# The second expert pass of an attention, MLP and expert-mixture kernel in hand-written program order

## The chip, the cores and the metric

The kernel runs on one core of a Trainium2 chip, in one launch. The time is device time in microseconds (us). TensorE (PE) multiplies, VectorE (DVE), ScalarE (ACT) and GpSimd (POOL) do the elementwise work, and SyncE (SP) issues the transfers. Each engine takes the instructions of its own queue in the order in which they stand there, and waits for the results of others by semaphores.

## What is computed

```python
x = attention(q, k, v)                 # 4 x 8 heads, 576 tokens, 64 wide; k and v averaged over 8 rows first
h = x @ w_in;  g = where(h > 0, h, exp(min(h, 0)) - 1);  x = g @ w_out       # 2304 x 512, inner 2048
P = exp(x @ w_gate - max);  8 times: P /= P.sum(1); P /= P.sum(0); P *= N / E
for e in range(8):                     # w1[e] 512 x 1024, w2[e] 1024 x 512
    out += P[:, e:e+1] * (np.maximum(x @ w1[e], 0.0) @ w2[e])
```

The change concerns the loop over the eight experts alone.

## The kernel before

Every float32 product is made of three products on a faster type, fp32r: an operand is cast to a high part ("hi", an ACT cast), the rest is subtracted into a low part ("lo", on POOL or DVE), and hi x hi, hi x lo and lo x hi are added up in PSUM. Each expert's two matrix products are blocked two by two and done by a scheme of seven block products with sums of blocks instead of eight.

**Pass 1** (the experts' first layer) runs over 32 pairs, an expert and a quarter of its hidden rows each, and within a pair over three units of 384 token columns. A unit has seven products of six matmuls (`Unit.product`, L810). The names in the trace: `pa` to `pd` are the PSUM banks of products, `m`, `u`, `r`, `s` the tiles that `Unit.read` makes of them, `w` the weights (`w10_31` is the high, `w11_31` the low half of pair 31's), `xs` the tokens. The results `r` and `s` are written to DRAM (`hid`) by `keep`, seven blocks of a unit. `split_pair(i)` makes a pair's weights: four sums and three subtractions (L781) on POOL, three casts on ACT (L780).

**The second pass** (the experts' second layer) runs over 72 pairs: 8 experts x 3 units x 3 blocks of 128 tokens. A pair has seven products of twelve matmuls 128x256 (`Pair.product`, L987), in the order a, b, then the seventh product of the pair before (c), then a, b, c, d. `prepare` makes a product's operands from the hidden blocks `hl` that come back from DRAM: the cast g (L954), in three of seven products a copy `pg` into PSUM (L957), and the low half g (L960), on POOL for two of the seven and on DVE for the others. It runs four products ahead of TensorE (`AHEAD`). `Pair.read` empties the banks: the copy n (L1014, ACT), the sums v, pc and poc (DVE), and the gated addition into the output tiles `acc` (in expert 0 ACT writes them, L1002; later DVE adds, L1004).

Beside an expert's pairs the next expert's weights are made: `weights_ahead` is a generator, and each call of `advance()`, one for each product of a pair, goes on with it to its next `yield`. `load_w2` fetches four blocks of 512 KB into two tiles `rv`. For each half of the rows there are seven blocks: B11, B22, B21 as they were loaded, and T1 to T4, which are differences of them (`sum_w2`, L906, POOL; three overwrite `rv`, the fourth, T3, has a tile `t3`). Each block is cast (L913, ACT) and its low half subtracted (L915, POOL).

Tiles come from pools: 24 large ones (`slot`: weights, tokens, `hl`, `rv`, `acc`), 13 small ones (`piece`: g, t3, n, v, and in pass 1 m, u, r, s), 8 PSUM banks (`bank`). A tile asked for when all are taken waits for the oldest to be given back. Only the attention's beginning stands in an order written by hand; from there on, in both passes of the experts too, a scheduler sets the order of each engine's queue.

Of the kernel before, what the change touches and what calls it, by code (L numbers as in the profile page):

```python
# [17 lines left out]
def tile_attention_mlp_moe(  # L18
# [31 lines left out]
    nc = tc.nc  # L50
# [30 lines left out]

    cpool = ctx.enter_context(tc.tile_pool(name="cpool", bufs=1))
    spool = ctx.enter_context(tc.tile_pool(name="spool", bufs=24))
    hpool = ctx.enter_context(tc.tile_pool(name="hpool", bufs=13))
    dpool = ctx.enter_context(tc.tile_pool(name="dpool", bufs=1, space=bass.MemoryType.DRAM))
    small = ctx.enter_context(tc.tile_pool(name="small", bufs=3))
    psum = ctx.enter_context(tc.tile_pool(name="psum", bufs=8, space=bass.MemoryType.PSUM))
# [700 lines left out]
    class Unit:  # L788
# [33 lines left out]
        def read(self, m):  # L822
            p = self.bank
            if m == 1:
                self.m1 = self.temp("m1")
                nc.scalar.copy(self.m1, p["a"])  # L826
            elif m == 6:
                self.u2 = self.temp("u2")
                nc.vector.tensor_add(self.u2, p["b"], self.m1)  # L829
            elif m == 2:  # L830
                self.r11 = self.temp("r11")
                nc.scalar.activation(self.r11, p["a"], AF.Relu)
                self.keep(H11, self.r11)
            elif m == 7:
                self.u3 = self.temp("u3")
                nc.vector.tensor_add(self.u3, p["b"], self.m1)
            elif m == 5:
                self.r22 = self.temp("r22")
                nc.vector.tensor_add(self.r22, p["c"], self.u3)  # L839
                nc.scalar.activation(self.r22, self.r22, AF.Relu)  # L840
                self.keep(H22, self.r22)
            elif m == 4:
                self.r12 = self.temp("r12")
                nc.vector.tensor_add(self.r12, p["d"], self.u3)
                nc.scalar.activation(self.r12, self.r12, AF.Relu)
                self.keep(H12, self.r12)
            else:

                c, s2 = p["c"], bank(f"ps_{self.i}_{self.u}")[:, 0:UW]
                s3 = self.temp("s3")  # L850
                nc.vector.tensor_add(c, c, self.u2)
                nc.vector.scalar_tensor_tensor(
                    s3, c, 0.0, self.r11, op0=ALU.max, op1=ALU.subtract
                )
                self.keep(HS3, s3)
                nc.vector.scalar_tensor_tensor(
                    c, c, 0.0, self.r22, op0=ALU.max, op1=ALU.add
                )
                nc.vector.tensor_sub(s2, c, self.r11)
                nc.scalar.copy(self.r22, c)  # L860
                self.keep(HS1, self.r22)
                nc.vector.tensor_sub(self.r12, self.r12, s2)
                self.keep(HS4, self.r12)
                nc.scalar.copy(self.r11, s2)
                self.keep(HS2, self.r11)


    w2s, loaded, prepared, acc = {}, {}, {}, {}
# [4 lines left out]


    B11, T2, B21, T3, T1, T4, B22 = range(7)
    ORDER2 = (1, 6, 2, 7, 5, 4, 3)
    LOADS2 = (range(0, 4), range(4, 7))

# [19 lines left out]
    def sum_w2(e, j, half):  # L898

        a, b = {T3: (T1, B22), T1: (T1, B11), T2: (B22, T1), T4: (B21, T2)}[j]  # L900
        if j == T3:
            out = sums2[e, half] = piece([P, 2, HF], F32, f"t3_{e}_{half}")
        else:
            raw2[e, j] = raw2[e, a]
            out = half_of(raw2[e, j], half)
        nc.gpsimd.tensor_sub(out, half_of(raw2[e, a], half), half_of(raw2[e, b], half))  # L906
# [13 lines left out]
    def weights_ahead(e):  # L920

        load_w2(e)
        for _ in range(8):
            yield
        for half in range(2):
            for j in (B11, B22, T3, B21, T1, T2, T4):
                if j in (T3, T1, T2, T4):
                    sum_w2(e, j, half)
                    yield
                yield from split_w2(e, j, half, nc.gpsimd)  # L930
                yield

    at_chunk2 = [0]

# [253 lines left out]
        while not all(k in made for k in CUTS if k[1] == u):  # L1188
            advance()

    def split_now(j, eng):
        for half in range(2):
            run(split_w2(0, j, half, eng))

    def first_weights(u):

        if u == 0:
            split_now(B11, nc.vector)
            split_now(B22, nc.vector)
            for j in (T3, T1, T2):  # L1200
                for half in range(2):
                    sum_w2(0, j, half)
        elif u == 1:
            del xslots[0]
            load_hidden()
            split_now(T2, nc.gpsimd)
            split_now(B21, nc.vector)
            split_now(T3, nc.gpsimd)
            split_now(T1, nc.gpsimd)
            for half in range(2):  # L1210
                sum_w2(0, T4, half)
        else:
            del xslots[1]
            load_hidden()
            load_hidden()
            split_now(T4, nc.gpsimd)

    def end_pair(p):
        p.product(6)
# [8 lines left out]
    for n, (i, u) in enumerate(order1):  # L1228
        need(u)
        unit = Unit(i, u)  # L1230
        for m in (1, 6, None, 2, 7, 5, 4):
            if m is not None:
                unit.product(m)
                unit.read(m)
            elif last is not None:
                last.product(3)
                last.read(3)
                if last.u == NUNIT - 1:
                    del w1s[last.i]
                if i == len(pairs) - 1:  # L1240
                    first_weights(u)
            advance(2 if len(made) < len(CUTS) else 1)
        last = unit
        if n == 2 * NUNIT - 2:
            need(NUNIT - 1)
            load_pair(2)
            load_pair(3)
        if n >= 2 * NUNIT - 1 and u == NUNIT - 1 and i + 1 < len(pairs):
            split_pair(i + 1)
            if i + 3 < len(pairs):  # L1250
                load_pair(i + 3)
        if (i, u) == (len(pairs) - 2, NUNIT - 1):
            load_w2(0)
    last.product(3)
    last.read(3)
    xslots.clear()
    w1s.clear()


    AHEAD = 4  # L1260
    N2 = len(pairs2)


    order2 = [(n + (j == 6), (0, 1, 3, 4, 5, 6, 2)[j], n, j) for n in range(N2) for j in range(7)]
    order2 = [7 * n + j for _, _, n, j in sorted(order2)]
    coming = iter(order2)
    for _ in range(AHEAD):
        prepare(next(coming))

    def prepare_next():  # L1270
        advance()
        i = next(coming, None)
        if i is not None:
            prepare(i)

    before = None
    for n in range(N2):
        e, u, s = pairs2[n]
        pair = Pair(n)
        for j in (0, 1, None, 2, 3, 4, 5):  # L1280
            if j is not None:
                prepare_next()
                pair.product(j)
                pair.read(j)
            else:
                if before is not None:
                    prepare_next()
                    end_pair(before)
                if e + 1 < E and (u, s) == (0, 0):
                    side.append(weights_ahead(e + 1))  # L1290
        before = pair
    end_pair(before)


# [33 lines left out]
```

## Time and profile before

| | us |
|---|---|
| median of 3 runs | 2031.45 (2029.45 to 2032.22) |
| profiled execution | 2033.06 |
| its span | 2031.30 |
| TensorE busy in it | 1950.4 (96%) |
| VectorE, ScalarE, GpSimd busy | 1360.8, 1101.2, 725.5 |

The second pass takes the span from 1235.8 to the end. The granted clock in the profile is 1 at 2.4 GHz, TensorE's higher level, and is lower where part of a stretch ran at the lower level of 1.2 GHz. A row of the timeline gives in brackets how long the engine had idled before the instruction and which instruction ended the wait; "issue" means that nothing visible did. Instructions follow each other in a pipeline, so a row's own time can reach into the next row's.

### The profile page before, as it was taken

What the parts mean: (1) busy time and instruction counts of PE and PEld (TensorE: products, weight loads), DVE (VectorE), ACT (ScalarE), POOL (GpSimd) and SP (SyncE); (2) the same over time, 40 slices, a digit from 0 to 9 for tenths busy, and PEclk for the clock granted to TensorE, in tenths of its full rate; (3) what the DMA queues carried; (4) which work ended last, traced back from release to release, by engine and by line L of the source; (5) the groups of instructions that cost most, each with busy time, mean ns of one, the idle gap of its engine ahead of it and who ended that gap; (6) DMA issues with size and microseconds to landing.
All of it is one profiled execution on the core that took longest, in us unless ns stands there. A gap on an engine that the chain in (4) does not pass through costs nothing. (4 is left out here: it accounts for less than half of the span.)

```text
span 2031.3 us, 35842 instructions
## 1 busy us (share of the span) xinstructions
PE 1950.4 (96%) x12717; PEld 1851.9 (91%) x12717; DVE 1360.8 (67%) x2586; ACT 1101.2 (54%) x2211; POOL 725.5 (36%) x624
## 2 busy tenths in 40 slices
PE   7799999999999999999999998898999999999999
PEld 4578888888999999999999998898989999999998
DVE  8687878445787666666666665556666666666666
ACT  5665545344444444444444446765666565656654
POOL 6510000020043233233233326645555554546422
PEclk7999999999999999999999999999999999999999
DMA  9221111000256656656656669675767676766691
GB/s 255 72 79 63 63 42 53 1 11 1 99 202 220 212 205 228 211 202 231 213 198 228 220 226 295 171 202 157 212 177 192 182 196 177 204 175 194 195 293 58
DMA packets 440163, 335.84 MB, mean 165 GB/s; under 512 B 25520, under 2 KB 431024, under 8 KB 439984
## 3 DMA queue, kind: packets, MB, share of 16 engines
q1 hardware_dynamic: 439984, 333.56, 53.2%
q8 instruction: 100, 1.64, 0.3%
q14 instruction: 79, 0.65, 0.1%
HBM read 196.62 MB, written 136.84 MB: 164 GB/s over the span
## 5 line engine op out<-in xcount | busy, mean ns | idle before, releaser
L954 ACT CAST g<-hl 128x512 fp32r<-128x512 f32 x504 | 305.2, 620 | 164.0 <-PE pob L987 83.1
L960 POOL TENSOR_TENSOR g<-hl,g 128x512 fp32r<-128x512 f32 x144 | 187.2, 1300 | 335.5 <-ACT g L954 266.0
L987 PE MATMUL pob<-w,g 128*128 128x256 f32 x1728 | 242.0, 291 | 17.1 <-POOL g L960 16.4
L781 POOL TENSOR_TENSOR w<-rw,w 128x512 fp32r<-128x512 f32 (+1 forms) x96 | 140.9, 1499 | 327.2 <-ACT w L780 259.1
L987 PE MATMUL poa<-w,g 128*128 128x256 f32 x1728 | 236.1, 287 | 16.0 <-ACT n L1014 13.5
L987 PEld LDWEIGHTS pob<-w,g 128*128 128x128 f32 x1728 | 227.0, 199 | 18.9 <-POOL g L960 17.9
L987 PE MATMUL poc<-w,g 128*128 128x256 f32 x1728 | 237.1, 287 | 7.1 <-DVE pc L1025 6.8
L987 PEld LDWEIGHTS poa<-w,g 128*128 128x128 f32 x1728 | 221.3, 195 | 18.1 <-ACT n L1014 15.1
L810 PE MATMUL pc<-xs,w 128*128 128x384 f32 x1152 | 231.9, 335 | 2.2 <-DVE r L839 2.2
L810 PE MATMUL pa<-xs,w 128*128 128x384 f32 x1152 | 231.6, 335 | 2.1 <-ACT m L826 2.1
L810 PE MATMUL pb<-xs,w 128*128 128x384 f32 x1152 | 231.2, 334 | 0.3 <-DVE u L829 0.3
L987 PEld LDWEIGHTS poc<-w,g 128*128 128x128 f32 x1728 | 223.0, 196 | 8.7 <-ACT w L913 7.6
L650 PE MATMUL p<-h,w 128*128 128x512 f32 (+1 forms) x960 | 215.9, 372 | 0.4 <-ACT h L638 0.4
L810 PEld LDWEIGHTS pa<-xs,w 128*128 128x128 f32 x1152 | 203.0, 188 | 3.1 <-ACT m L826 3.1
L775 POOL TENSOR_TENSOR rw<-rw 128x256 f32<-128x256 f32 x32 | 23.9, 747 | 507.9 <-DMA rw<-in_moe_w_dram 415.1
L960 DVE TENSOR_TENSOR g<-pg,g 128x512 fp32r<-128x512 f32 x216 | 148.7, 688 | 84.4 <-ACT g L954 39.4
L810 PEld LDWEIGHTS pc<-xs,w 128*128 128x128 f32 x1152 | 201.8, 188 | 3.4 <-DVE r L839 3.4
L810 PEld LDWEIGHTS pb<-xs,w 128*128 128x128 f32 x1152 | 202.2, 188 | 1.4 <-DVE u L829 1.4
L650 PEld LDWEIGHTS p<-h,w 128*128 128x128 f32 x960 | 167.6, 190 | 29.9 <-ACT h L638 0.6
L617 PE MATMUL p<-xh,w 128*128 128x512 f32 x512 | 171.8, 395 | 0.0
L960 DVE TENSOR_TENSOR g<-hl,g 128x512 fp32r<-128x512 f32 x144 | 117.6, 817 | 38.2 <-ACT g L954 15.4
L829 DVE TENSOR_TENSOR u<-pb,m 128x384 f32<-128x384 f32 x96 | 53.4, 557 | 133.1 <-PE pb L810 65.1
(152 smaller groups left out, 3318.4 us busy)
## 6 DMA issues: line engine op xcount, KB each, us to landing
hl<-hid SPq DMA_DIRECT2D x504, 256.0 KB, 5.1
hid<-r SPq DMA_DIRECT2D x576, 192.0 KB, 2.5
hid<-s SPq DMA_DIRECT2D x96, 192.0 KB, 2.1
rw<-in_moe_w_dram SPq DMA_DIRECT2D x128, 128.0 KB, 2.7
rv<-in_moe_w_dram SPq DMA_DIRECT2D x32, 512.0 KB, 6.9
raw<-in_moe_w_in_dram SPq DMA_DIRECT2D x16, 512.0 KB, 4.1
raw<-in_moe_w_out_dram SPq DMA_DIRECT2D x16, 512.0 KB, 11.2
vraw<-in_v_dram SPq DMA_DIRECT2D x16, 288.0 KB
```

Source lines behind the costliest of these rows:

```text
L617: nc.tensor.matmul(ps[:, 0:n], wc[:, 0, a, c * P : (c + 1) * P], b[:, c, :], start=c == 0 and m == 0, stop=c == NC - 1 and m == 2,)
L650: nc.tensor.matmul(ps[j][:, 0 : WIDTH[t]], wc[:, 1, a, j * P : (j + 1) * P], h[b], start=f == 0 and m == 0, stop=f == SIZE[g] - 1 and m == 2,)
L775: g.tensor_sub(raw[:, S3], raw[:, A11], raw[:, A21])
L781: g.tensor_sub(w1s[i][1][:, js], raw[:, rs], f32(w1s[i][0][:, js]))
L810: nc.tensor.matmul(self.bank[b], a[:, c, :], x, start=first and c == 0 and n == 0, stop=c == 1 and n == 2, skip_group_check=not first,)
L829: nc.vector.tensor_add(self.u2, p["b"], self.m1)
L954: nc.scalar.copy(hi, x)
L960: eng.tensor_sub(lo, x, f32(hi))
L987: nc.tensor.matmul(self.bank[b], h[a][:, f, :], w2s[self.e, j][:, l, f, :], start=first and f == 0 and n == 0, stop=f == NPAIR - 1 and n == 2,
```

## The change

Five edits. (1) The second pass stands in a `manual_schedule` block for all five engines: each engine's queue is in the order in which the code issues the instructions. (2) `weights_ahead` has more `yield`s: a sum is followed by two, and a block without a sum has one more at its end, so that 58 steps stand where 44 stood; `load_w2(0)` is called earlier (before `split_pair(31)`). (3) From expert 1 on, T3 goes into the free half of the last output tile (`acc_t3`), not into a piece; the small pool has 14 tiles. (4) The last three results of a unit of pass 1 go to new pieces `s1`, `s4`, `s2` and no longer overwrite r22, r12 and r11. (5) The first expert's weights are a generator stepped once for each step of pass 1's last pair, where they were issued in three lumps, and the operands of the second pass's first four products are prepared ahead of pass 1's last product.

```diff
-    hpool = ctx.enter_context(tc.tile_pool(name="hpool", bufs=13))
+    hpool = ctx.enter_context(tc.tile_pool(name="hpool", bufs=14))
...
                 nc.vector.tensor_sub(s2, c, self.r11)
-                nc.scalar.copy(self.r22, c)
-                self.keep(HS1, self.r22)
-                nc.vector.tensor_sub(self.r12, self.r12, s2)
-                self.keep(HS4, self.r12)
-                nc.scalar.copy(self.r11, s2)
-                self.keep(HS2, self.r11)
+                v = self.temp("s1")
+                nc.scalar.copy(v, c)
+                self.keep(HS1, v)
+                v = self.temp("s4")
+                nc.vector.tensor_sub(v, self.r12, s2)
+                self.keep(HS4, v)
+                v = self.temp("s2")
+                nc.scalar.copy(v, s2)
+                self.keep(HS2, v)
...
         if j == T3:
-            out = sums2[e, half] = piece([P, 2, HF], F32, f"t3_{e}_{half}")
+            if e == 0:
+                out = piece([P, 2, HF], F32, f"t3_{half}")
+            else:
+                out = half_of(spare[0], half)
+            sums2[e, half] = out
...
             for j in (B11, B22, T3, B21, T1, T2, T4):
-                if j in (T3, T1, T2, T4):
+                if j in SUMS:
                     sum_w2(e, j, half)
+                    yield
                     yield
                 yield from split_w2(e, j, half, nc.gpsimd)
                 yield
+                if j not in SUMS:
+                    yield
+
+    spare = []
+
+    def last_acc():
+
+        both = slot([P, SLOT], F32, "acc_t3")
+        half = SLOT // 2
+        acc[NTILE - 1] = both[:, 0:half].rearrange("p (s d) -> p s d", d=DM)
+        spare.append(both[:, half:SLOT].rearrange("p (f d) -> p f d", f=NPAIR))
...
+    def first_weights():
+
+
+        G, V = nc.gpsimd, nc.vector
+        sum_w2(0, T3, 0), split0(B11, None, V)
+        yield
+        sum_w2(0, T3, 1), split0(B11), split0(B22, None, V)
+        yield
+        sum_w2(0, T1, 0), split0(B22)
+        yield
+        sum_w2(0, T1, 1)
+        yield
+        sum_w2(0, T2, 0)
+        yield
+        sum_w2(0, T2, 1)
+        yield
+        yield
+        del xslots[0]
+        load_hidden()
+        split0(T2, None, G), split0(B21, None, V)
+        yield
+        split0(B21), split0(T2, 0)
...
                 if last.u == NUNIT - 1:
                     del w1s[last.i]
-                if i == len(pairs) - 1:
-                    first_weights(u)
+                if (i, u) == (len(pairs) - 2, NUNIT - 1):
+                    load_w2(0)
+                if (i, u) == (len(pairs) - 1, 0):
+                    side.append(first_weights())
...
-        if (i, u) == (len(pairs) - 2, NUNIT - 1):
-            load_w2(0)
-    last.product(3)
-    last.read(3)
...
+    for _ in range(AHEAD):
+        prepare(next(coming))
+
+    last.product(3)
+    last.read(3)
+    xslots.clear()
+    w1s.clear()
+    last_acc()
+
+
+    with tc.manual_schedule(engines={E_.PE, E_.DVE, E_.Activation, E_.Pool, E_.SP}):
+        before = None
+        for n in range(N2):
```

What this does to the queues stands in the order of the two programs. First POOL's queue while the weights of expert 3 are made beside expert 2, in the kernel before: `w2_3_*` are low halves of weights, `rv3_*` sums, `g1_*` low halves of the pairs' operands; a name in brackets is an engine or transfer queue that the instruction waits for.

```order
L960 TENSOR_TENSOR g1_162_16145<-hl23_0_16015,g0_162_16144 128x512 [waits DMAHW5_49,PE_49,Activation_49]
L906 TENSOR_TENSOR t3_3_1_16162<-rv3_0_15513,rv3_6_15516 128x512 [waits DVE_49,PE_49]
L906 TENSOR_TENSOR rv3_0_15513<-rv3_0_15513 128x512 [waits Pool_49]
L906 TENSOR_TENSOR rv3_6_15516<-rv3_6_15516,rv3_0_15513 128x512 [waits Pool_49]
L915 TENSOR_TENSOR w2_3_3_15795<-t3_3_1_16162,w2_3_3_15795 128x512 [waits Activation_49]
L915 TENSOR_TENSOR w2_3_4_15904<-rv3_0_15513,w2_3_4_15904 128x512 [waits Activation_49]
L906 TENSOR_TENSOR rv3_6_15516<-rv3_6_15516 128x512 [waits Pool_49]
L915 TENSOR_TENSOR w2_3_1_15970<-rv3_6_15516,w2_3_1_15970 128x512 [waits Activation_49]
L915 TENSOR_TENSOR w2_3_5_16035<-rv3_6_15516,w2_3_5_16035 128x512 [waits Activation_49]
L960 TENSOR_TENSOR g1_165_16236<-hl23_1_16063,g0_165_16235 128x512 [waits DMAHW0_49,PE_49,Activation_49]
```

The same place of the changed kernel:

```order
L980 TENSOR_TENSOR g1_162_16423<-hl23_0_16294,g0_162_16422 128x512 [waits DMAHW5_49,DVE_49,Activation_49]
L923 TENSOR_TENSOR w2_3_5_16464<-rv3_6_15802,w2_3_5_16464 128x512 [waits DMAHW3_49,DMAHW2_49,Activation_49]
L980 TENSOR_TENSOR g1_165_16513<-hl23_1_16341,g0_165_16512 128x512 [waits DMAHW0_49,DVE_49,Activation_49]
L923 TENSOR_TENSOR w2_3_0_15968<-rv3_0_15799,w2_3_0_15968 128x512
L980 TENSOR_TENSOR g1_169_16573<-hl24_0_16444,g0_169_16572 128x512 [waits DMAHW4_49,DVE_49,Activation_49]
L923 TENSOR_TENSOR w2_3_6_16034<-rv3_6_15802,w2_3_6_16034 128x512
L914 TENSOR_TENSOR acc_t3_13062<-rv3_0_15799,rv3_6_15802 128x512
L980 TENSOR_TENSOR g1_172_16661<-hl24_1_16492,g0_172_16660 128x512 [waits DMAHW7_49,DVE_49,Activation_49]
L923 TENSOR_TENSOR w2_3_3_16137<-acc_t3_13062,w2_3_3_16137 128x512 [waits Activation_49]
L980 TENSOR_TENSOR g1_176_16722<-hl25_0_16595,g0_176_16721 128x512 [waits DMAHW3_49,DVE_49,Activation_49]
L923 TENSOR_TENSOR w2_3_2_16185<-rv3_6_15802,w2_3_2_16185 128x512
L914 TENSOR_TENSOR rv3_0_15799<-rv3_0_15799 128x512
```

Before, eight weight steps stand between g1_162 and g1_165; in the changed kernel no more than two stand between one g1 and the next, and T3's sum (`acc_t3`) waits for nothing.

Then TensorE's queue where pass 1's last pair (31) begins, in the kernel before:

```order
L810 MATMUL pa_31_0_12444<-xs0_0_3974,w10_31_12430 128x384 x2
L810 MATMUL pa_31_0_12444<-xs0_0_3974,w11_31_12431 128x384 [waits Pool_49]
L810 MATMUL pa_31_0_12444<-xs0_0_3974,w10_31_12430 128x384 x2
L810 MATMUL pa_31_0_12444<-xs0_0_3974,w11_31_12431 128x384
L810 MATMUL pb_31_0_12453<-xs0_3_3977,w10_31_12430 128x384 x2
L810 MATMUL pb_31_0_12453<-xs0_3_3977,w11_31_12431 128x384 [waits Pool_49]
L810 MATMUL pb_31_0_12453<-xs0_3_3977,w10_31_12430 128x384 x2
L810 MATMUL pb_31_0_12453<-xs0_3_3977,w11_31_12431 128x384
L810 MATMUL pc_30_2_12404<-xs2_1_4745,w10_30_12190 128x384 [waits DVE_49]
L810 MATMUL pc_30_2_12404<-xs2_2_4746,w10_30_12190 128x384
L810 MATMUL pc_30_2_12404<-xs2_1_4745,w11_30_12191 128x384
L810 MATMUL pc_30_2_12404<-xs2_1_4745,w10_30_12190 128x384
```

The same place of the changed kernel:

```order
L810 MATMUL pa_31_0_12720<-xs0_0_3974,w10_31_12712 128x384 x2
L810 MATMUL pb_31_0_12729<-xs0_3_3977,w10_31_12712 128x384 x2
L810 MATMUL pc_30_2_12686<-xs2_1_4745,w10_30_12457 128x384 [waits DVE_49]
L810 MATMUL pc_30_2_12686<-xs2_2_4746,w10_30_12457 128x384
L810 MATMUL pc_30_2_12686<-xs2_1_4745,w11_30_12458 128x384
L810 MATMUL pc_30_2_12686<-xs2_1_4745,w10_30_12457 128x384
L810 MATMUL pc_30_2_12686<-xs2_2_4746,w10_30_12457 128x384
L810 MATMUL pc_30_2_12686<-xs2_1_4745,w11_30_12458 128x384
L810 MATMUL pa_31_0_12720<-xs0_0_3974,w11_31_12713 128x384 [waits Pool_49]
L810 MATMUL pa_31_0_12720<-xs0_0_3974,w10_31_12712 128x384 x2
L810 MATMUL pa_31_0_12720<-xs0_0_3974,w11_31_12713 128x384
L810 MATMUL pb_31_0_12729<-xs0_3_3977,w11_31_12713 128x384 [waits Pool_49]
```

Before, twelve matmuls of pair 31 stand ahead of pc_30_2, the last product of the pair before. In the changed kernel four stand there, and the others, which need the low half w11_31, stand behind it.

Last ACT's queue ahead of m1_31_2, the copy of the first product of pass 1's last unit, in the kernel before (`w2_0_5` is the cast of T4):

```order
L860 COPY r22_31_0_12523<-pc_31_0_12516 128x384 [waits DMAHW7_49,DVE_49,Activation_49]
L864 COPY r11_31_0_12505<-ps_31_0_12562 128x384 [waits DMAHW1_49,DVE_49]
L840 ACTIVATE r22_31_1_12626<-r22_31_1_12626 128x384 [waits DMAHW4_49,DVE_49]
L845 ACTIVATE r12_31_1_12637<-r12_31_1_12637 128x384 [waits DMAHW5_49,DVE_49]
L826 COPY m1_31_2_12648<-pa_31_2_12641 128x384 [waits PE_49]
L913 CAST w2_0_5_12687<-rv0_6_12441 128x512 [waits Pool_49]
L913 CAST w2_0_5_12687<-rv0_6_12441 128x512
```

The same place of the changed kernel:

```order
L921 CAST w2_0_4_12917<-rv0_0_12663 128x512
L921 CAST w2_0_5_12967<-rv0_6_12666 128x512 [waits PE_49,Pool_49]
L867 COPY s2_31_0_12854<-ps_31_0_12841 128x384 [waits DMAHW2_49,DVE_49]
L832 ACTIVATE r11_31_1_12874<-pa_31_1_12816 128x384 [waits DMAHW5_49,DMAHW7_49,DMAHW3_49,PE_49]
L921 CAST w2_0_5_12967<-rv0_6_12666 128x512 [waits Pool_49]
L826 COPY m1_31_2_12927<-pa_31_2_12920 128x384 [waits DMAHW1_49,PE_49,Activation_49]
L840 ACTIVATE r22_31_1_12899<-r22_31_1_12899 128x384 [waits DMAHW5_49,DVE_49]
```

Before, both casts of T4 stand behind m1_31_2; in the changed kernel both stand ahead of it, each with a wait for POOL.

## Rows read from the trace of the kernel before

**Rows 1.** Page, part 1: busy us, share of the span, instructions of each engine.

```profile
PE 1950.4 (96%) x12717; PEld 1851.9 (91%) x12717; DVE 1360.8 (67%) x2586; ACT 1101.2 (54%) x2211; POOL 725.5 (36%) x624
```

**Rows 2.** Windows by stretch; PE, PEld, DVE, ACT, POOL busy, clock, DMA share, GB/s.

```profile
700.00:1120.00 420.00, 420.00 (x2425) 420.00 (x2424) 271.20 (x520) 199.14 (x404) 140.69 (x137) 1.00 0.61 215
...
1235.80:1250.75 14.95, 11.80 (x72) 11.01 (x73) 7.55 (x15) 9.48 (x20) 3.86 (x3) 0.77 0.96 307
1250.75:1340.57 89.82, 83.55 (x674) 82.40 (x673) 45.08 (x81) 64.77 (x127) 51.28 (x38) 0.98 0.71 199
1340.57:1933.98 593.41, 561.99 (x4538) 558.51 (x4538) 384.80 (x700) 364.47 (x681) 319.44 (x240) 0.97 0.69 189
1933.98:2014.62 80.64, 80.64 (x674) 80.64 (x673) 55.57 (x104) 47.03 (x88) 20.81 (x16) 1.00 0.67 193
```

**Rows 3.** Waits of PE, second pass: us in total, times, longest us.

```profile
PE pob L987 <- POOL g L960: 16.4, 7, 2.9
PE poa L987 <- ACT n L1014: 13.5, 8, 2.3
PE poc L987 <- DVE pc L1025: 6.8, 8, 1.2
```

**Rows 4.** Windows: the 3.4 us behind one wait (columns of the second group).

```profile
1474.90:1478.30 3.40, 3.39 (x17) 3.39 (x18) 2.38 (x5) 1.81 (x4) 3.40 (x3) 0.55 0.48 138
```

**Rows 5.** Timeline of POOL in expert 2: start, us, instruction [idle before it].

```profile
1461.72 1.30 POOL L906 TENSOR_TENSOR t<-rv,rv 128x512 f32<-128x512 f32 x1 [4.15 <-issue]
...
1490.66 1.30 POOL L960 TENSOR_TENSOR g<-hl,g 128x512 fp32r<-128x512 f32 x1 [2.03 <-DVE g L960]
...
1503.05 1.30 POOL L960 TENSOR_TENSOR g<-hl,g 128x512 fp32r<-128x512 f32 x1
```

**Rows 6.** Timeline of ACT and PE, the same stretch, two windows.

```profile
1474.91 2.50 PE L987 MATMUL pob<-w,g 128*128 128x256 f32 x10 [2.58 <-POOL g L960]
...
1500.64 0.62 ACT L913 CAST w<-rv 128x512 fp32r<-128x512 f32 x1 [2.32 <-POOL rv L906]
...
1502.11 1.70 PE L987 MATMUL poa<-w,g 128*128 128x256 f32 x12 [1.73 <-ACT n L1014]
```

**Rows 7.** Groups by line and form, second pass: busy us, mean ns, idle before.

```profile
L960 DVE TENSOR_TENSOR g<-pg,g 128x512 fp32r<-128x512 f32 x216 | 148.7, 688 | 84.4 <-ACT g L954 39.4 <-ACT pg L957 24.9 <-POOL w L915 5.7
...
L960 DVE TENSOR_TENSOR g<-hl,g 128x512 fp32r<-128x512 f32 x144 | 117.6, 817 | 38.2 <-ACT g L954 15.4 <-ACT pg L957 13.9 <-issue 1.6
...
L915 POOL TENSOR_TENSOR w<-rv,w 128x512 fp32r<-128x512 f32 x84 | 115.2, 1386 | 27.1 <-ACT w L913 22.7 <-PE pod L987 2.5 <-issue 1.5
```

**Rows 8.** Waits of ACT in pass 1, of 420 us.

```profile
ACT r L860 <- DMA hid<-r: 19.7, 19, 1.9
```

**Rows 9.** Timeline of POOL, then of PE, end of pass 1.

```profile
1208.85 2.55 POOL L906 TENSOR_TENSOR t<-rv,rv 128x512 f32<-128x512 f32 x2 [13.10 <-ACT r L860]
...
1217.29 1.29 POOL L906 TENSOR_TENSOR rv<-rv,rv 128x512 f32<-128x512 f32 x1 [3.40 <-DVE w L915]
1219.27 1.27 POOL L906 TENSOR_TENSOR rv<-rv,rv 128x512 f32<-128x512 f32 x1 [0.69 <-DVE w L915]
...
1227.67 1.29 POOL L906 TENSOR_TENSOR rv<-rv 128x512 f32<-128x512 f32 x1
...
1212.07 1.20 PE L810 MATMUL pc<-xs,w 128*128 128x384 f32 x6
...
1220.30 1.32 PE L810 MATMUL pc<-xs,w 128*128 128x384 f32 x6 [0.78 <-DVE r L839]
1222.45 1.31 PE L810 MATMUL pa<-xs,w 128*128 128x384 f32 x6 [0.83 <-ACT m L826]
...
1229.84 1.20 PE L810 MATMUL pa<-xs,w 128*128 128x384 f32 x6
```

**Rows 10.** Group of POOL's line L781, wide form.

```profile
L781 POOL TENSOR_TENSOR w<-rw,w 128x768 fp32r<-128x768 f32 x4 | 7.4, 1853 | 41.5 <-ACT w L780 23.6 <-PE pc L810 17.8
```

More of the change, by code (lines that the diff above doesn't have):

```diff
@@ L875, in tile_attention_mlp_moe @@
     B11, T2, B21, T3, T1, T4, B22 = range(7)
+    SUMS = (T1, T2, T3, T4)
     ORDER2 = (1, 6, 2, 7, 5, 4, 3)
@@ L1189, in need, with split0 @@
             advance()
[L1191 to L1216, printed above, removed]
+    splitting = {}
+    def split0(j, half=None, eng=None):
+        for h in range(2) if half is None else (half,):
+            if (j, h) in splitting:
+                run(splitting.pop((j, h)))
+            else:
+                splitting[j, h] = split_w2(0, j, h, eng)
+                next(splitting[j, h])
+    def first_weights():
[18 more added lines that the diff above has]
+        split0(B21), split0(T2, 0)
+        yield
+        split0(T2, 1), split0(T3, None, G)
+        yield
+        sum_w2(0, T4, 0), split0(T3, 0)
+        yield
+        sum_w2(0, T4, 1), split0(T1, None, G)
+        yield
+        split0(T3, 1)
+        yield
+        split0(T1, 0)
+        yield
+        del xslots[1]
+        load_hidden()
+        split0(T1, 1), split0(T4, None, G)
+        load_hidden()
+        yield
+        split0(T4, 0)
+        yield
+        split0(T4, 1)
     def end_pair(p):
@@ L1251, in tile_attention_mlp_moe @@
                 load_pair(i + 3)
-        if (i, u) == (len(pairs) - 2, NUNIT - 1):
-            load_w2(0)
-    last.product(3)
-    last.read(3)
-    xslots.clear()
-    w1s.clear()
+    while side:
+        advance()
     AHEAD = 4
@@ L1266, in tile_attention_mlp_moe @@
     coming = iter(order2)
-    for _ in range(AHEAD):
-        prepare(next(coming))
     def prepare_next():
@@ L1274, in prepare_next @@
             prepare(i)
[L1276 to L1286, printed above, removed]
-                    prepare_next()
[L1288 to L1292, printed above, removed]
+    for _ in range(AHEAD):
[8 more added lines that the diff above has]
+        for n in range(N2):
+            e, u, s = pairs2[n]
+            pair = Pair(n)
+            for j in (0, 1, None, 2, 3, 4, 5):
+                if j is not None:
+                    prepare_next()
+                    pair.product(j)
+                    pair.read(j)
+                else:
+                    if before is not None:
+                        prepare_next()
+                        end_pair(before)
+                    if e + 1 < E and (u, s) == (0, 0):
+                        side.append(weights_ahead(e + 1))
+            before = pair
+        end_pair(before)
 _INS = ["q", "k", "v", "moe_w_in", "moe_w_out", "moe2_w_gate", "moe2_w1", "moe2_w2"]
```

## The prediction

> **What bounds the kernel now.** I read the page's busy line first, then the windows by stretch, then the waits of TensorE, and last the timelines of POOL, ACT and PE around two of those waits. TensorE is busy for 96% of the span [rows 1], so a gain can come only from stretches in which it idles or runs at the lower clock, and the windows show where these are [rows 2]. Pass 1 has none: in 420 us TensorE is busy for 420 us at the full granted clock (1.00, 2.4 GHz). The last expert has none either: eight pairs in 80.64 us, 10.08 us a pair. That is the price of a pair that waits for nothing, since 84 matmuls stand in it and 80.64 us over 672 of them is 0.12 us each. The six experts between take 593.41 us for 6 x 9 = 54 pairs; at 10.08 these would be 544.32 us, so **49.1 us** are lost there, 8.2 us an expert. Expert 0 loses 89.82 - 80.64 = **9.2 us** in its pairs 1 to 8. The first pair takes 14.95 us at a clock of 0.77, **4.9 us** too much.
>
> What the lost time is made of is in the waits of TensorE in the second pass [rows 3]: one on POOL's low half g in seven experts (16.4 us), one on the copy n by ACT (13.5 us in 8 cases), one on pc of DVE (6.8 us in 8). The rest is the clock: in the 3.4 us behind the first of these in expert 2 the granted clock is 0.55, where TensorE, having stood for about 2.6 us, runs at its lower level (1.2 GHz) most of the time [rows 4]. That gives 0.45 x 3.4 = 1.5 us for such a dip.
>
> The last expert differs from the others in one thing, that no weights are prepared beside it. Its engines: DVE 55.57, ACT 47.03, POOL 20.81 of 80.64 us. In experts 1 to 6 they are busy for 384.80, 364.47 and 319.44 us [rows 2]; over a quiet 544.32 us this would be 71, 67 and 59%. No engine is full; what makes TensorE wait is the order. The timelines show it [rows 5, 6]. POOL's sum t stands at its queue's head from 1457.6 to 1461.72 without starting ("issue", 4.15 us): its output is a piece of the small pool, whose place has to come free. What stood behind it then runs in a lump, and TensorE's pob waits 2.58 us for the g behind that. In the weights' second half POOL ends a g at 1491.96 and starts the next at 1503.05: eight weight steps lie between. ACT's cast of a weight waits 2.32 us for one of the sums; the copy n stands behind it, and TensorE's poa waits for n, 1.73 us.
>
> **The change part by part.**
>
> *Order and spreading (second pass).* No instruction of a quiet pair is added or removed; the work per expert stays 14 casts, 8 sums and 14 subtractions. In the order of the changed kernel POOL has at most two weight steps between two g, where eight stood. Two steps and a g are 2 x 1.39 + 1.30 = 4.1 us [rows 5, 7]. The operands are made four products ahead of TensorE, 4 x 1.44 = 5.76 us. So a g is never the last thing to come, with 1.7 us over. Every cast of a summed weight now stands at least two product steps (2.88 us) behind its sum, which takes 1.30 us [rows 5]; so ACT should not stand at such a cast with n behind it. And t3, from expert 1 on, goes into a half tile of its own that nothing else uses, so the 4.15 us at the head of POOL's queue go. SP's transfers stand in the same order in these pairs, so the loaded tiles come when they came. What is late next: nothing that I find by rows. Per pair ACT has 10.08 - 364.47 / 54 = 3.3 us over, DVE 2.9, POOL 4.2. Taken: all 49.1 us of experts 1 to 6 go. Ends: none of it (the waits stay), or all of it. Value: the end at the last expert's row, since the engines' sums fit.
>
> *Expert 0, pairs 1 to 8.* The same three waits and the same cure, though ACT, which writes the gated rows there, is at 64.77 of 89.82 us. In 80.64 us that is 80%, 2.0 us over per pair. Taken: -9.2; ends 0 and -9.2.
>
> *The first pass's copies.* Before, the last two copies and one subtraction of a unit overwrite tiles that a DMA is still reading, and wait for it, ACT's L860 for 19.7 us over 420 us [rows 8]. TensorE is full at that place, so the wait lies wholly beside it: 0, and it cannot be a gain in pass 1. One more buffer a pool changes nothing else there.
>
> *The end of pass 1.* Here I expect a loss. The first expert's weights are now loaded before the last pair's first-layer weights take their tiles, and both come from the same 24 slots. In the changed order the low half w11_31 gets the tile that w10_30 held, so POOL can begin it only when the previous pair's last product has read w10_30 for the last time; TensorE's rows show the result, two matmuls of pa and pb ahead of pc_30_2 where twelve stood, then a pa that waits for POOL. By the rows of before [rows 9, 10]: pc_30_2 started at 1212.07; eight matmuls (420 us by 2425 of them, 0.173 us each [rows 2]) fewer ahead make it 1210.7, its fifth ends at 1211.6. POOL then takes 1.85 us for the first subtraction; TensorE has one matmul left, so pa waits 1.7 us, and pb, needing the next piece (128x512, 1.30 us like the g [rows 5]) and having four matmuls (0.69 us) in front, 0.6 more: 2.3 us.
> POOL's chain of sums begins behind three such pieces (4.45 us), at 1216.0 instead of 1208.85. It had 3.40 + 0.69 us of waiting for DVE in it, which the later start covers, so it runs 7.2 - 4.1 = 3.1 us late. One more subtraction (1.37 us) now stands ahead of the second sum of T4, which ended at 1228.96: now 1233.4. Behind it on ACT stand its cast (0.62 [rows 6]) and then m1_31_2 (three quarters of that), which stood ahead of it before: 1234.4. TensorE needs m1_31_2 at 1229.84 + 2.3, less the two waits of before that these replace (0.78 and 0.83): 1230.5. It waits 3.9 us. Sum: 2.3 + 3.9 - 1.6 = **+4.6** (ends 0, if the slot clash costs nothing because the hi halves cover it, and +8).
>
> *The first pair.* Before ACT can write n1_0, it now has s1 and s2 of the last unit and a cast before it, and these wait for a chain of four DVE operations on 128x384. By width, from the 688 ns for 128x512 and the 0.62 us cast [rows 6, 7], an estimate: chain 4 x 0.52, copy 0.47, cast 0.62, n 0.31, together 3.5 us and some hand-overs between engines, against 2 x 1.44 us of products that cover it: about 1 us of wait, and as much again on the product behind. I take **+2.2** (ends -4.9, if the first pair becomes quiet, and +5). And the waits of 2.3 and 3.9 us in a stretch that had none above 0.83 [rows 9] are each long enough for a dip like the one seen [rows 4]: 1.5 to 1.7 us each, less what the first pair's own dip may overlap: **+2.5** (0 to 3.4).
>
> Sum, against the profiled execution (2033.06 us, its span 2031.30): 2033.06 - 49.1 - 9.2 + 4.6 + 2.2 + 2.5 = 1984.1. The median of the runs (2031.45) lies 1.6 us below the profiled one, so the forecast is **1982.5 us**, 2.4% faster.
>
> **The rivals.**
> *A: one wait an expert stays.* By hand, program order is exact, and an order that puts one g or one n behind a late cast does so in every expert. Price: 2 to 3 us of wait and a dip of 1.5, about 4 us in each of six experts: 24 us, so 2006. For it: three sorts of wait stand in the list, of which two hang on POOL and ACT, but pc on DVE has no reason of its own in my reading. Against it: it comes only where the others have upset the order.
> *B: the change does not do what it says.* Before, the scheduler put the instructions almost as program order does; if the lump is not what makes TensorE wait, all 58.3 us stay and the end of pass 1 costs its 9.3: 1982.5 + 58.3 = 2041, slower. For it: in quiet pairs the order of the two kernels is nearly the same. Against it: both long waits end with POOL's or ACT's weight steps [rows 5, 6].
> *C: DVE becomes the bound.* DVE's subtraction from the loaded tile takes 817 ns on the mean, and 688 where one operand comes from PSUM [rows 7]; POOL's own run beside it. Spread over all pairs, POOL's steps would meet both of a pair's two such subtractions, each time for up to a step of 1.39 us: 2.8 us a pair, against 2.9 us that DVE has over. It decides from there on: slower than before needs 0.74 us a pair beyond what is over (53 us over 72 pairs). At 1 us a pair the time is 1982.5 + 72 = 2055. For it: 817 against 688. Against it: POOL's sum of work is the same as before, and TensorE met DVE only at pc, 6.8 us in all.
> The Trainium skill, "SBUF — State Buffer", section "Who interferes with whom", says that a DVE instruction with two inputs in SBUF and a GpSimd instruction that reads SBUF exclude each other for a whole instruction, whoever comes first. By that rule the 817 is the mean of blocked and free ones, and C is its outcome if the spreading makes meetings the rule; the trace agrees with the rule so far as the form with a PSUM operand is the faster one, and does not decide how often they would meet.
>
> **How the numbers follow.** Forecast 0.68, A 0.16, B 0.08, C 0.08. A time within 0.2% (4 us, about what a measurement of this kernel can tell from no change) of 2031.45 comes only from between A and B: 0.03 from both. So faster 0.87, same 0.03, slower 0.10. The likeliest case's own range is 1973 (pass 1's end and first pair cost nothing) to 1992 (they cost twice as much). Below, the first pair's 4.9 us may go too: 1968. Above, A is to be taken in: 2008.
>
> **What would show it.** Right: each of experts 1 to 6 at about 90.7 us with 758 matmuls, the clock 1.00 from about 1265 on; no wait on POOL's g or on n in TensorE's list there; no "issue" ahead of POOL's t; at the end of pass 1 a pa that waits for POOL's L781 for about 1.7 us and one for ACT's m for about 4. Wrong: waits of 2 to 3 us once an expert (A), the lump's waits still there (B), pairs of 11 us or more in every expert with TensorE waiting for DVE (C), or a pass 1 that ends where it did before.

## The result, and the profile after

The changed kernel takes **1982.91 us** (median of 4 runs, 1982.17 to 1986.09), the kernel before 2031.84 (4 runs, 2029.45 to 2035.16): ratio 0.9761 with a 95% interval of 0.9743 to 0.9779, 2.4% faster. The forecast was 1982.5. The span went from 2031.3 to 1981.6 us.

The windows by stretch of the changed kernel's trace (columns as in [rows 2]) are the second pass's first pair, the next nine pairs (expert 0's other eight and one of expert 1), and 54 pairs that take in experts 1 to 6.

```profile
1241.60:1258.45 16.85, 11.48 (x73) 10.90 (x73) 7.98 (x15) 8.38 (x17) 3.84 (x3) 0.80 1.09 346
1258.45:1350.11 91.66, 91.41 (x758) 90.86 (x757) 50.56 (x89) 68.76 (x139) 54.82 (x40) 1.00 0.72 201
1350.11:1894.43 544.32, 544.32 (x4539) 544.32 (x4537) 393.82 (x705) 359.08 (x680) 314.53 (x241) 1.00 0.74 204
```

In 544.32 us TensorE is busy for 544.32 us at the full clock, 10.08 us a pair, which is the quiet price of [rows 2] to the digit. The same 54 pairs of the kernel before, and its nine ahead of them, from its trace:

```profile
1250.77:1350.70 99.93, 93.66 (x759) 92.51 (x757) 50.75 (x92) 72.15 (x142) 53.88 (x40) 0.98 0.75 210
1350.70:1944.08 593.38, 561.96 (x4539) 558.48 (x4538) 386.05 (x702) 362.95 (x679) 319.45 (x240) 0.97 0.69 189
```

593.38 - 544.32 = 49.1 us came from the 54 pairs, 99.93 - 91.66 = 8.3 from the nine. Against that the second pass begins at 1241.60 and not 1235.87 (+5.7), and the first pair takes 16.85 us, 1.95 more than before. -49.1 - 8.3 + 5.7 + 1.95 = -49.7, the difference of the spans. The waits of TensorE from 1150 us to the end (us in total, times, longest):

```profile
PE poa L1007 <- ACT n L1034: 5.4, 2, 5.2
PE pa L810 <- ACT m L826: 2.9, 1, 2.9
PE pa L810 <- POOL w L781: 1.9, 1, 1.9
PE pb L810 <- POOL w L781: 0.7, 1, 0.7
PE pc L810 <- DVE r L839: 0.3, 1, 0.3
PE pob L1007 <- POOL g L980: 0.2, 1, 0.2
```

Of the three rows of [rows 3], 36.7 us, one wait of 0.2 us on POOL's g and two on n are left: 5.16 us in the first pair and 0.25 us near the end of expert 0. In experts 1 to 6 TensorE waits for nothing. POOL's timeline in expert 2, the place of [rows 5]:

```profile
1484.28 1.29 POOL L980 TENSOR_TENSOR g<-hl,g 128x512 fp32r<-128x512 f32 x1 [2.71 <-ACT g L974]
1485.53 1.30 POOL L923 TENSOR_TENSOR w<-rv,w 128x512 fp32r<-128x512 f32 x1
1487.39 1.30 POOL L980 TENSOR_TENSOR g<-hl,g 128x512 fp32r<-128x512 f32 x1 [0.56 <-ACT g L974]
1488.65 1.30 POOL L923 TENSOR_TENSOR w<-rv,w 128x512 fp32r<-128x512 f32 x1
1489.90 1.75 POOL L914 TENSOR_TENSOR acc_t<-rv,rv 128x512 f32<-128x512 f32 x1
```

One or two weight steps lie between two g, the sum `acc_t` starts without a wait, and POOL now waits for casts of ACT.

### The profile page after: what moved, and what is told of

Its sections match the earlier page's. It is cut to its first block, busy times and chain, and to the rows that moved or that the text cites. A ratio compares the mean times of both kernels' runs of the same rounds, so it can differ in the third digit from the quotient of the medians.

```text
span 1981.6 us, 35832 instructions
## 1 busy us (share of the span) xinstructions
PE 1930.6 (97%) x12717; PEld 1838.6 (93%) x12717; DVE 1384.9 (70%) x2586; ACT 1087.7 (55%) x2211; POOL 722.4 (36%) x624
## 5 line engine op out<-in xcount | busy, mean ns | idle before, releaser
L781 POOL TENSOR_TENSOR w<-rw,w 128x512 fp32r<-128x512 f32 (+1 forms) x96 | 141.3, 1504 | 338.0 <-ACT w L780 250.6
L1007 PE MATMUL pob<-w,g 128*128 128x256 f32 x1728 | 232.0, 284 | 0.2 <-POOL g L980 0.2
L1007 PE MATMUL poc<-w,g 128*128 128x256 f32 x1728 | 230.8, 283 | 0.0
L1007 PEld LDWEIGHTS pob<-w,g 128*128 128x128 f32 x1728 | 218.8, 193 | 0.4 <-POOL g L980 0.4
L1007 PEld LDWEIGHTS poc<-w,g 128*128 128x128 f32 x1728 | 217.7, 192 | 0.0
L861 ACT COPY s<-pc 128x384 f32<-128x384 f32 x96 | 46.1, 480 | 235.0 <-issue 203.8
```

What stands on the lines that cost most here:

```text
L781: g.tensor_sub(w1s[i][1][:, js], raw[:, rs], f32(w1s[i][0][:, js]))
L861: nc.scalar.copy(v, c)
L1007: nc.tensor.matmul(self.bank[b], h[a][:, f, :], w2s[self.e, j][:, l, f, :], start=first and f == 0 and n == 0, stop=f == NPAIR - 1 and n == 2,
```

## The experiments

Four theories stood to be told apart: the gain is the program order's; it is the spread of the weight steps; it is T3's own tile; and, for the end of pass 1, the loss is the slot of w11_31, or something else. In each kernel nothing is changed but what its diff shows; each was timed against the kernel before on its chip.

**The changed kernel without program order (e1).**

```diff
-    with tc.manual_schedule(engines={E_.PE, E_.DVE, E_.Activation, E_.Pool, E_.SP}):
+    if True:
         before = None
```

> The changed kernel with only its second pass given back to the scheduler (spread weight steps, acc_t3 and the new end of pass 1 stay). POOL's queue then has lumps of 8 and 4 weight steps between two g again, where program order has at most 2. Order theory: the waits of TensorE on POOL's g, on n and on pc come back in every expert, 6 to 8 us each: 2025 to 2035 us. Spreading theory: what counts is where the steps are issued, the time stays near 1983 to 1990.

Measured 2049.71 us, ratio 1.0091 (1.0077 to 1.0104): slower than before, and 67 us slower than with the block. From its trace the 54 pairs (window), TensorE's wait in the second pass, and POOL's over some five experts:

```profile
1355.71:1958.84 603.13, 560.77 (x4539) 558.54 (x4537) 370.59 (x703) 359.25 (x673) 305.60 (x236) 0.96 0.66 185
```

```profile
PE poc L1007 <- POOL g L980: 48.1, 14, 6.1
```

```profile
POOL acc_t L914 <- DMA rv<-in_moe_w_dram: 31.4, 5, 6.5
```

The scheduler put T3's sum where its data had not landed, POOL stood there for 6 us an expert, and a lump followed. So the extra `yield`s bring nothing when the scheduler sets the order: 603.13 against 593.38 us. The time lies outside both theories' ranges, and of the three waits only the one on g came back. T3's own tile stays in this kernel, and how much of the loss is owed to it no run shows.

**The kernel before with program order alone (e2).** The diff is the `with` line around before's loop over the pairs and its indentation.

> The kernel before with program order in the second pass and nothing else (44 weight steps, t3 in a piece, old copies, old end of pass 1). POOL has up to 3 weight steps between two g: 3 x 1.39 + 1.30 = 5.5 us against a lead of 5.76, and a cast stands one step behind its sum. Order theory: experts go quiet as in the changed kernel (-57 us), and the loss of 5.7 us at the end of pass 1 isn't there: 1973 to 1980, below the changed kernel. Spreading theory: one wait of 1 to 3 us and a clock dip an expert stay: 1990 to 2010. If program order without the new t3 stops POOL: 4 us an expert more, 2000 or above.

Measured 2003.45 us, ratio 0.9862 (0.9848 to 0.9875). **The changed kernel with before's steps (e3):**

```diff
                 if j in SUMS:
                     sum_w2(e, j, half)
                     yield
-                    yield
                 yield from split_w2(e, j, half, nc.gpsimd)
                 yield
-                if j not in SUMS:
-                    yield
```

> The changed kernel with the 44 weight steps of before in place of 58 (a cast one step behind its sum, up to 3 steps between two g). Order theory: same as the changed kernel within 0.3% (1980 to 1988). Spreading theory: a wait on n or g in each of six experts, 1 to 4 us each: 1990 to 2007.

Measured 2003.16 us, ratio 0.986 (0.9847 to 0.9874). The nine and the 54 pairs of e2, then of e3:

```profile
1251.46:1353.57 102.11, 93.61 (x758) 92.38 (x757) 53.11 (x89) 69.74 (x139) 54.51 (x40) 0.98 0.72 198
1353.57:1914.92 561.35, 549.65 (x4538) 545.61 (x4537) 391.01 (x705) 357.39 (x680) 332.04 (x240) 1.00 0.72 196
```

```profile
1259.19:1359.86 100.67, 93.61 (x758) 92.58 (x757) 53.34 (x89) 70.10 (x140) 54.51 (x40) 0.98 0.68 190
1359.86:1914.63 554.77, 546.54 (x4539) 544.99 (x4538) 391.20 (x705) 353.03 (x679) 328.46 (x240) 1.00 0.72 199
```

ACT's waits for the weights' sums in one expert of e3, then its only wait at such a cast in one expert of the changed kernel, which is not for a sum:

```profile
ACT w L921 <- POOL rv L914: 13.6, 6, 2.8
...
ACT w L921 <- POOL acc_t L914: 3.6, 1, 3.6
```

```profile
ACT w L921 <- DVE g L980: 1.9, 1, 1.9
```

The order theory's range failed in both kernels. Both times lie in the spreading theory's ranges, but spreading is not the whole either: order by itself brings 593.38 - 561.35 = 32.0 us of the 49.1, and nothing in expert 0 (102.11 against 99.93). Nor does T3's piece stop POOL in this order. In e2 it waits ahead of t for 1.5 us in six cases, 0.3 us at most, where the kernel before has 22.5 us of "issue" in six. With before's steps a cast comes one product behind its sum, and ACT stands at seven casts an expert for 17.2 us; n is behind, and TensorE loses (554.77 - 544.32) / 6 = 1.7 us an expert in e3 and 100.67 - 91.66 = 9.0 us in expert 0, where ACT also writes the gated rows. With two products between them ACT waits for no sum at all. The spread steps are worth 20 us (e3 against the changed kernel), but only in program order. Between e2 and e3 lie another 561.35 - 554.77 = 6.6 us in the 54 pairs. They differ in T3's tile, the small pool's 14th tile, the copies and the end of pass 1, and no run parts these while the steps are before's.

**T3 in pieces (e5).** In `sum_w2` the branch `if e == 0` is taken for every expert.

> The changed kernel with T3 in a piece of the small pool for every expert (its 14 pieces rotate; the half tile acc_t3 isn't used). Theory that program order and the spread steps do the whole: same time, 1981 to 1987, and no 'issue' ahead of POOL's t. Rival, that t3's tile was what let the lump go: POOL stands about 4 us at t twice an expert, a g comes late, 2 to 4 us an expert: 1995 to 2008.

Measured 1983.36 us (1983.08 to 1983.60), ratio 0.9755 (0.9742 to 0.9769), and one wait of TensorE behind the first pair, 0.2 us on n as in the changed kernel. T3's tile is worth nothing in this order with the spread steps. The 4.15 us of "issue" in [rows 5] came of where the scheduler had put the sum: here and in e2 it uses a piece too, and POOL does not stand at it.

**The copies of pass 1 at their old places (e6)**, `Unit.read` as it was before.

> The changed kernel with the last three results of a unit of pass 1 back in r22, r12 and r11. Theory that the copies' places cost and gain nothing in pass 1 (TensorE is full there): the second pass's start within 1 us of the changed kernel's, and the time 1981 to 1986; n1_0 still takes the tile of the store s3_31_2, so its wait of 5 us stays. Rival, that the new places hide stores which now stop DVE and ACT: 1987 to 1995.

Measured 1983.04 us, ratio 0.9754 (0.974 to 0.9767): no difference, as expected. The second pass starts 2.0 us sooner (1239.60), where at most 1 us was expected, but n's wait is 1.1 us longer (6.3), and the span is the same (1981.4 us).

**The first weights loaded later (e4).**

```diff
-                if (i, u) == (len(pairs) - 2, NUNIT - 1):
-                    load_w2(0)
...
                 load_pair(i + 3)
+        if (i, u) == (len(pairs) - 2, NUNIT - 1):
+            load_w2(0)
```

> The changed kernel with load_w2(0) back behind split_pair(31), as before, and nothing else. The low half w11_31 then takes the tile of w10_29 and not of w10_30, and n1_0 takes the tile of g0_0, not that of s3_31_2 (a store). Theory that the slot clash makes the loss: the pa and pb waits on L781 (1.86 and 0.73 us) go with the dip behind them (1.9), the m1_31_2 wait (2.9 and a dip) shrinks, the n wait loses its last 2.45 us: 1971 to 1977. Rival, that the two tiles' transfer, now later, holds the sums back: the m1 wait grows by as much as the others fall: 1980 to 1986.

Measured 1983.43 us, ratio 0.9764 (0.9751 to 0.9778): nothing gained, as the rival said. TensorE's waits at the end of pass 1 and in the first pair, from its trace:

```profile
PE pa L810 <- ACT m L826: 4.3, 2, 3.0
PE poa L1007 <- ACT n L1034: 3.0, 2, 2.6
PE pob L1007 <- DVE v L1037: 2.5, 1, 2.5
PE pc L810 <- DVE r L839: 2.1, 2, 1.6
```

The waits on L781 are gone, yet m1's is 3.0 us as it was and pc's grew from 0.3 to 2.1. The second pass starts at 1241.35, against 1241.60. The slot was not what set the end: POOL's chain of sums ends only 1.0 us sooner (1232.6 for 1233.6), and ACT waits for it with m1_31_2 behind. And n's wait fell to 2.6 while one on v (2.5) appeared. ACT's next cast behind n waits 1.98 us for a store (`hid<-s`), DVE's g waits for ACT, and v stands behind that g.

**The last pair in program order too (e7, e8).** To e4's edit is added a `manual_schedule` block from pass 1's last pair on; in e8 DVE also makes s1 and s2 of the very last unit.

> The changed kernel with load_w2(0) back behind split_pair(31) and pass 1's last pair, too, in program order. ACT's m1_31_2 then stands ahead of both casts of T4, and n1_0 takes the tile of g0_0. Theory that the loss at the end of pass 1 is ACT's queue (casts waiting for POOL's sums, m1 behind them), not the slot: the m1 wait of 2.9 us and its dip go, n's wait falls to about 2.5: 1974 to 1979. Rival, that POOL's chain of sums sets the end whatever stands on ACT (the first products of the second pass wait for w2_0 instead): 1981 to 1986.

> As the kernel with the last pair by hand, and the two copies s1 and s2 of pass 1's very last unit are made by DVE and not ACT, so that ACT's n1_0 has no instruction ahead of it that waits for DVE's chain. Theory that this chain makes n1_0 late: its wait goes, 1970 to 1976, 2 to 5 below the kernel with the copies on ACT. Rival, that DVE's own queue now makes v2 late (two copies of 0.56 us more ahead of it): the wait moves from n to v and the time stays within 1 us of that kernel.

Measured 1986.10 us, ratio 0.9769 (0.9755 to 0.9782), and 1985.95, ratio 0.977 (0.9757 to 0.9783): no gain. Program order put m1_31_2 ahead of T4's casts, but also DVE's r behind two low halves of weights, of which the first waits 2.11 us for ACT's cast, and n's wait stayed at 5.4 us. In e8 n's wait is 4.6 us and v's 2.6, so e8's rival held. TensorE's waits in e7:

```profile
PE poa L1007 <- ACT n L1034: 5.6, 2, 5.4
PE pc L810 <- DVE r L839: 3.9, 2, 2.6
```

**Two edits at the joint (e9 to e11).** In e9 n1, v2 and v3 of the first pair lie in the free half tile; e10 adds that T4 of expert 0 is split behind n1; e11 adds e8's copies on DVE.

```diff
         def temp(self, name):
+            if self.n == 0:
+                return spare[0][:, ("n1", "v2", "v3").index(name), :]
             return piece([P, HF], F32, f"{name}_{self.n}")
...
-        split0(T1, 1), split0(T4, None, G)
+        split0(T1, 1)
         load_hidden()
-        yield
-        split0(T4, 0)
-        yield
-        split0(T4, 1)
...
                     prepare_next()
+                    if (n, j) == (0, 1):
+                        split0(T4, None, nc.gpsimd), split0(T4)
                     pair.product(j)
```

> The changed kernel, and n1, v2 and v3 of the second pass's first pair lie in the half tile acc_t3 (which nothing else uses until expert 1's T3) and not in pieces that stores of pass 1's last unit still read. Theory that about half of n's wait of 5.16 us is a piece held by the store of s3_31_2 (ACT idle for 2.45 us ahead of n): the wait falls to about 2.7, and v waits for no store: 1978 to 1981. Rival, that the stores only move on to the next piece (g0_5 behind n on ACT takes it): 1982 to 1985, with the wait on g or v in its place.

> As the kernel with pair 0's own tile, and T4 of the first expert is cast and subtracted behind n1_0 and not in pass 1's last unit, so that ACT's m1_31_2 has no cast that waits for POOL ahead of it. Theory that m1's wait of 2.9 us and its dip (1.5) are these casts' doing: they go, 1974 to 1978. Rival, that POOL's chain of sums sets the end through the other weights: no gain over the kernel with the own tile alone, or a wait for w2_0_5 in pair 0: 1978 to 1984.

> As the kernel with pair 0's own tile and T4 behind n, and the copies s1 and s2 of pass 1's very last unit are made by DVE. Theory that ACT's place behind DVE's chain is the other half of n's wait: it goes too, 1972 to 1976. Rival, that v (DVE, behind two more copies) takes its place: within 1 us of the kernel without.

Measured: e9 1982.89 us, ratio 0.9754 (0.9741 to 0.9767); **e10 1978.77 us**, ratio 0.9737 (0.9724 to 0.975); e11 1978.85, ratio 0.9736 (0.9723 to 0.9749). TensorE's waits in e9, e10 and e11, then ACT's cast behind n in e9 and TensorE's first row of the second pass in e10:

```profile
PE poa L1007 <- ACT acc_t L1036: 3.3, 1, 3.3
PE pa L810 <- ACT m L826: 3.0, 1, 3.0
...
PE pob L1007 <- DVE acc_t L1039: 1.4, 1, 1.4
```

```profile
PE poa L1007 <- ACT acc_t L1036: 2.6, 1, 2.6
PE pob L1007 <- DVE acc_t L1039: 2.1, 1, 2.1
PE pa L810 <- POOL w L781: 1.9, 1, 1.9
```

```profile
PE pob L1009 <- DVE acc_t L1041: 3.8, 1, 3.8
...
PE poa L1009 <- ACT acc_t L1038: 1.6, 1, 1.6
```

```profile
1250.98 0.62 ACT L974 CAST g<-hl 128x512 fp32r<-128x512 f32 x1 [2.15 <-DMA hid<-s]
```

```profile
1236.63 0.42 PE L1007 MATMUL poa<-w,g 128*128 128x256 f32 x2
```

In e10 m1's wait is gone, with the waits on L781 still there. The second pass starts at 1236.63, 5.0 us sooner than in the changed kernel. Of that 0.4 us was there already at the pa that waits for L781 (1211.87 against 1212.31), so the edit is worth about 4.5 us. T4's cast and subtraction ahead of m1_31_2 were thus most of the 5.7 us lost at the end of pass 1. e10 and e11, which share this edit, are the only kernels here below the changed one. e10 takes 4.1 us less than e9, timed beside it (the runs' ranges, 1977.54 to 1981.43 and 1981.22 to 1983.23, overlap by 0.2).

The first pair's wait for n fell from 5.2 to 3.3 us in e9, but 1.4 came on v instead, and in e11 n's fell to 1.6 and v's rose to 3.8: it moves between ACT and DVE and stays near 5 us. In e9 ACT no longer idles ahead of n, but the cast behind it waits 2.15 us for a store, DVE's g waits for ACT, and v stands behind that g. So the store only moved on to the next piece, as the rival of e9 said. How much of the sum is owed to DVE's chain for pass 1's last unit was not settled.

**The next weights' load one pair later (e12)**: `(u, s) == (0, 0)` becomes `(u, s) == (0, 1 if e == 0 else 0)` where `weights_ahead` is started.

> The changed kernel with the load of expert 1's weights (2 MB) and their steps begun one pair later; nothing else. Theory that the stores of pass 1's last unit land late because that load shares the transfer engines with them: n's wait falls by 1 to 2.4 us, 1980 to 1982. Rival, that they are late for the loads of hl, or wait for DVE: unchanged at 1983; and if the weights come too late for expert 1, a wait of some us at its first pair: 1985 or above.

Measured 1983.99 us, ratio 0.976 (0.9747 to 0.9774): the load is not why n waits; its wait is 5.8 us, where 1 to 2.4 us less was to come if the load delayed the stores.

## Why the prediction was right

**The sum.** In the spans the two gains are 49.1 + 8.3 = 57.4 us where 58.3 was forecast, and the losses where the passes join 5.7 + 1.95 = 7.7 us where 9.3 was. The mechanism of the gain was right. That the median lies within 0.4 us of the forecast is luck: 0.9 us too much gain and 1.6 us too much loss, which nearly cancel.

**What bounds, and the second pass.** The step "all 49.1 us of experts 1 to 6 go" came out at 49.1, that of expert 0 at 8.3 for 9.2; the rest of it is 0.94 us in the last three of the nine pairs. The argument that the engines' sums fit and only the order makes TensorE wait was right, and e2 and e3 show that both halves of it were needed: the forecast gave order and spreading one answer. In this sequence order alone is worth 28 us, spreading as the last step 20. What it said of t3's tile was wrong: with order and spreading there, that tile is worth nothing (e5).

**The copies** were put at 0 and are worth 0 (e6).

**The end of pass 1.** The forecast was a loss of 4.6 us by waits of 2.3 and 3.9 us, and 2.5 for the clock. TensorE's timeline of the changed kernel, ACT's ahead of m1_31_2 and of n, and the window behind the wait on m:

```profile
1212.31 0.96 PE L810 MATMUL pa<-xs,w 128*128 128x384 f32 x4 [1.86 <-POOL w L781]
1214.00 1.37 PE L810 MATMUL pb<-xs,w 128*128 128x384 f32 x4 [0.73 <-POOL w L781]
...
1234.71 2.20 PE L810 MATMUL pa<-xs,w 128*128 128x384 f32 x6 [2.93 <-ACT m L826]
...
1250.49 2.93 PE L1007 MATMUL poa<-w,g 128*128 128x256 f32 x12 [5.16 <-ACT n L1034]
```

```profile
1233.66 0.62 ACT L921 CAST w<-rv 128x512 fp32r<-128x512 f32 x1 [2.30 <-POOL rv L914]
1234.18 0.47 ACT L826 COPY m<-pa 128x384 f32<-128x384 f32 x1
...
1250.06 0.37 ACT L1034 COPY n<-poa 128x256 f32<-128x256 f32 x1 [2.45 <-issue]
```

```profile
1234.71:1238.00 3.29, 3.29 (x11) 3.29 (x12) 3.07 (x6) 1.31 (x4) 2.62 (x3) 0.52 0.52 153
```

The waits are 1.86 + 0.73 on L781 (1.7 + 0.6 forecast) and 2.93 on m (3.9); the cast waits 2.30 us for the sum and m1 stands behind it. Each stands where it was expected, and the product behind m1's wait starts at 1234.71, 4.9 us behind the 1229.84 of [rows 9], for 4.6 forecast. But the waits don't add up as the forecast added them: e4 takes the first away and gains nothing, e10 takes the second away, leaves the first, and gains 4.5 us. The chain of POOL and ACT sets the end either way; the 2.3 us were not a price of their own. Nor is the slot the main reason that this chain is late: without it, in e4, the chain still ends at 1232.6, 3.6 us behind the kernel before (1228.96). The clock's term was too large. The dip behind m's wait costs 0.48 x 3.29 = 1.6 us, but the kernel before waits 0.67 us for an operand's cast at the start of the second pass, and the changed one does not; so 0.9 us is left of the 2.5.

**The first pair.** A loss of 2.2 us by n was forecast and 1.95 us is measured, but only in part for the reason given. Of the 5.16 us that TensorE waits for n, ACT idles 2.45 us ahead of n with nothing else to wait for ("issue"): by the order in which the tiles are handed out, its piece is the one that the store of s3_31_2 is reading. The gap is gone in e9, where n has a tile of its own. That store had no place in the forecast. Removing it from n (e9) takes 1.9 us off n's wait and gives 1.4 back on v. The prediction also took 10.08 us as the first pair's quiet price; that pair has six products, 72 matmuls, so 8.64 us, and its excess before was 6.3 us and not 4.9. Only the 1968 hangs on this.

**The rivals.** A (one wait an expert) is what e2 and e3 are, at 2.8 and 1.7 us an expert in the 54 pairs, and with no dip of the clock there (1.00); in the changed kernel it is not there. B is excluded by the waits. C's sign is in the trace, without its price: DVE's subtraction from the loaded tile went from the 817 ns of [rows 7] to 923, the one with a PSUM operand stayed at 684.

```profile
L980 DVE TENSOR_TENSOR g<-pg,g 128x512 fp32r<-128x512 f32 x215 | 147.1, 684 | 50.3 <-ACT pg L977 46.7 <-ACT g L974 0.6 <-POOL g L980 0.4
L980 DVE TENSOR_TENSOR g<-hl,g 128x512 fp32r<-128x512 f32 x144 | 132.9, 923 | 18.2 <-ACT g L974 12.4 <-issue 3.2 <-POOL rv L914 2.6
```

DVE is busy for 393.82 us in the 54 pairs, 386.05 before: 0.14 us a pair of the 2.9 it had over. The Trainium skill, "SBUF — State Buffer", section "Who interferes with whom", says that a DVE instruction with two inputs in SBUF contends with a GpSimd instruction that reads SBUF; the trace agrees on which form it hits. Program order makes this form slower, and not the spread steps: it takes 963 and 965 ns in e2 and e3, with before's steps, and 791 in e1, with the spread steps under the scheduler (windows 1260 to 1960 us, where the changed kernel has 931). The cost stays covered.

## What to carry to other kernels

Where no engine is full and the fastest still waits, look in the queues for instructions that stand at the head of a lump or directly behind the producer of their operand; a producer and its consumer on another queue want a step or two of other work between them, and that spacing holds only where the order is kept as it is written. Two waits that end at one chain are one price: take away each by itself before adding them. A small pool's next tile may be one that a transfer is still reading; the row shows as a wait with no visible releaser, or with the transfer as releaser, ahead of an instruction whose operands are there.

## What was not expected of the hardware

Stores of 192 KB around the start of the second pass landed late. From 1236 to 1255 us of the changed kernel the median from issue to landing is 4.5 us for s and 4.9 for r, where over the whole kernel before it is 2.1 and 2.5; s3 was ready at 1244.8, and n1, in its piece, started at 1250.06. From 1241.60 to 1258.45 the transfer engines' share is 1.09. The change did not bring this: from 1230 to 1252 us of the kernel before the median for r is 4.1 us. And behind a wait of 5.16 us TensorE's next twelve matmuls took 2.93 us at a granted clock of 0.50, the lower level, where such a row has 1.70 at the full clock [rows 6]; the first pair's mean clock is 0.80.
